# The epsilon of every layer norm added by VectorE instead of GpSimd, in a transformer block on one core

## The chip, the cores and the metric

The kernel runs on one core of a Trainium2 chip. The metric is the device time of one execution in microseconds (us), as the median of three runs. Five engines work side by side: TensorE (PE in the profile, its weight loads PEld), VectorE (DVE), ScalarE (ACT), GpSimd (POOL) and SyncE (SP), whose queue issues nearly all DMAs here. Each engine takes its instructions strictly in the order in which they were written, and waits on semaphores for the others.

## The reference

One block of a transformer over 2048 tokens of width 576, in bf16: a layer norm, an attention with 32 heads of width 18 in 4 segments of 512 tokens with a memory carried from segment to segment, a residual, a second layer norm, and a feed-forward network of width 4608 with gelu, and a second residual. Cut to what matters:

```
def _layernorm(x, axis=-1, eps=1e-05):
    m = mean(x); v = var(x)
    return (x - m) / sqrt(v + eps)

h   = x + A(_layernorm(x), wq, wk, wv, wo, beta)      # attention, 4 segments of 512 tokens
out = h + gelu(_layernorm(h) @ w1 + b1) @ w2 + b2
```

In A each segment s computes softmax(q k^T * scale + causal mask) v, mixed by a gate g = sigmoid(beta) with phi(q) M / (phi(q) z), where M and z sum phi(k)^T v and phi(k) over the segments before.

## The kernel before, in words

Tokens lie on the 128 partitions, so the 2048 tokens are 16 tiles of 128, four to a segment. Both layer norms are done tile by tile: 16 for the input x (stage X), 16 for h behind the attention (stage B), 32 in all.

The stages of a segment are X (layer norm of x and transposes to xreg; tiles of segment 0 and half of those of segment 1 are transposed on TensorE, L738, the others by DMA), P (projections to q, k, v, nine pairs of matmuls each, L835), A (scores L1002 and L1163, exponentials on ScalarE L1005 and L1167, masks on VectorE L1015 and L1176 or on GpSimd L1018 and L1178, values L1034 and L1189, block transposes on VectorE such as L1048, L1143 and L1197, and small normalising steps), M (the memory, L928), B (output projection L793 and L819, residual L1241, layer norm, transposes), C (first feed-forward matmul, L1301 and L1338, its evictions and the gelu) and D (second feed-forward matmul L1388, the last residual L1400, the store).

A layer norm of one tile is a small function, `layernorm` (L700 onward). It acquires one of six small buffers `ln` of 16 floats per partition and records three operations:

- `stats` on VectorE: two BN_STATS over the halves of 288 columns (L710) into columns 0 to 11, and a BN_AGGR (L711) that makes the mean (column 12) and the variance (column 13).
- `rstd` on GpSimd: a TENSOR_SCALAR (L714) that adds 1e-5 to the variance into column 14, and a TENSOR_TENSOR (L715) that raises column 14 to the power -0.5, read from the constant column `mhalf`, into column 15.
- `apply` on VectorE: subtracts the mean and multiplies by column 15 (L726). For the first two tiles of segment 0 it only subtracts the mean (L724), and the factor is put in where the projections are evicted (L628, L632).

What sets the order of the work: a table of numbers, TIMETABLE, which gives every operation an engine and a place in one global row. Operations are emitted in the order of these numbers. A small planner (`schedule`) walks the same row with the costs that stand in the code and picks which buffer of a set each operation gets; it does not reorder. The compiler adds the semaphore waits.

Of the kernel before, what the change touches and what calls it, by code (L numbers as in the profile page):

```python
# [12 lines left out]
ALU = mybir.AluOpType  # L13
# [357 lines left out]
class Graph:  # L371
# [12 lines left out]
    def add(self, prio, cost, fn, after=(), acq=None, use=(), table=None, size=0, name=""):  # L384
        key = self.tag + name
        n = self.count[key] = self.count.get(key, -1) + 1
        acq = [b for b in (acq if isinstance(acq, list) else [acq]) if b is not None]
        op = Op(prio, cost, fn, after, acq, [b for b in use if b is not None], table, size, name)
        op.tag = self.tag
        op.start, op.eng = self.timetable[key, n]  # L390
        for b in op.use + acq:
            b.left += 1
        self.ops.append(op)
        return op
# [66 lines left out]
def kernel(  # L461
# [11 lines left out]
    nc = tc.nc  # L473
# [15 lines left out]
    EPS = 1e-5  # L489
# [107 lines left out]
    def build():  # L597
# [4 lines left out]
        add = gr.add  # L602

        def memset(prio, eng, cost, *aps, val=0.0, after=()):
            def fn(e):
                for ap in aps:
                    if e == "act":
                        nc.scalar.memzero(ap)
                    else:
                        VEC[e].memset(ap, val)  # L610
            return add(prio, {eng: cost}, fn, after, name="memset")
# [38 lines left out]
        half_ok = memset(-9, "dve", 0.1, mhalf[:], val=-0.5)  # L650
# [53 lines left out]
        def layernorm(prio, src, after, xsrc, dst_buf, dcost, extra=(), centred=None):  # L704

            sm = Buf(ln_s)

            def stats(e):
                for c in range(2):
                    nc.vector.bn_stats(out=sm.t[:, 6 * c:6 * c + 6], in_=src()[:, c * HALF:(c + 1) * HALF])  # L710
                nc.vector.bn_aggr(out=sm.t[:, 12:14], in_=sm.t[:, 0:12].rearrange("p (a b) -> p a b", b=6))  # L711
            a = add(prio, {"dve": 1.06}, stats, after, sm, [xsrc], name="stats")
            def rstd(e):
                nc.gpsimd.tensor_scalar(out=sm.t[:, 14:15], in0=sm.t[:, 13:14], scalar1=EPS, scalar2=None, op0=ALU.add)  # L714
                nc.gpsimd.tensor_tensor(out=sm.t[:, 15:16], in0=sm.t[:, 14:15], in1=mhalf[:], op=ALU.pow)  # L715
            b = add(prio, {"pool": 0.92}, rstd, [a, half_ok], None, [sm], name="rstd")

            if centred is not None:
                rstd_of[centred] = sm, b

            def apply(e):
                w = src().shape[-1]
                if centred is not None:
                    VEC[e].tensor_scalar(out=dst_buf.t[:, 0:w], in0=src(), scalar1=sm.t[:, 12:13], scalar2=None, op0=ALU.subtract)  # L724
                    return
                VEC[e].tensor_scalar(out=dst_buf.t[:, 0:w], in0=src(), scalar1=sm.t[:, 12:13], scalar2=sm.t[:, 15:16], op0=ALU.subtract, op1=ALU.mult)  # L726
            return add(prio, {"dve": dcost}, apply, [a, b if centred is None else None] + list(extra), dst_buf, [sm, xsrc], name="apply")
# [15 lines left out]
        def stage_X(s, prio):  # L743
# [3 lines left out]
            for tl in range(TPS):  # L747
                gr.tag = f"X{s}{tl // 2 if s == 0 else ''}"
                if s == 0:
                    if tl == 1:  # L750
                        w_ok["q"] = load_w(-7.4, "q", 0)
                        xs_pre.append(load_x(-7.3, 2))
                        xs_pre.append(load_x(-7.2, 3, xs_pre[2][0]))
                        for op in (xs_pre[2][1], xs_pre[3][1], w_ok["q"][0]):
                            held(op).after.append(x_gate)
                    xb, ld = xs_pre[tl]
                elif tl % 2 == 0:
                    xb, ld = load_x2(prio + 0.1 * tl, s * TPS + tl, [applied[3]])
                xn = Buf(xn_s)
                pl = prio + 0.1 * tl if s == 0 else X_PRIO + 0.3 * s + 0.05 * tl  # L760
                ap = layernorm(pl, lambda xb=xb, tl=tl: xb.t[:, tl % 2, :], [ld] + ([xs_pre[0][1], x0b] if s == 0 else []), xb, xn, 0.50, [], tl if (s, tl) in CENTRED else None)
                applied.append(ap)
                if (s, tl // 2) not in PE_X:
                    wr[tl] = load(prio + 0.1 * tl, lambda tl=tl: xnd[s][tl * P:(tl + 1) * P, :], lambda xn=xn: xn.t[:], 164e3, [ap], use=[xn])
                    continue
                buf, j = bufs[tl // 2], tl % 2
                even = transposes(prio + 0.1 * tl, xn, [ap], lambda buf=buf, j=j: buf.t[:, 0:KT, j * P:(j + 1) * P],
                                  None if j else buf, [buf] if j else [], name="TX", one=0.06 if s or tl else 0.108)
                odd = transposes(prio + 0.1 * tl, xn, [ap], lambda buf=buf, j=j: buf.t[:, KT:ND, j * P:(j + 1) * P], None, [buf], ND - KT, name="TX", c0=64, one=0.06 if s or tl else 0.108)
                odd.after.append(even)  # L770
                if j:
                    even.after.append(xn_ok[s, tl - 1][0])
                xn_ok[s, tl] = [even, odd]
# [451 lines left out]
        def stage_B(s, prio):  # L1225
# [3 lines left out]
            for tl in range(TPS):  # L1229
# [9 lines left out]
                for hf, c in enumerate(cc):  # L1239
# [3 lines left out]
                        [c, xb] + ([] if hf == 0 else [h]), name="hadd")  # L1243
                xn2 = Buf(xn2_s)
                ap = layernorm(p0, lambda h=h: h.t[:], [prev], h, xn2, 0.62, later)
                ap = add(p0, {"pool": 0.29, "dve": 0.22}, lambda e, xn2=xn2: VEC[e].tensor_copy(out=xn2.t[:, D:XW], in_=xn2.t[:, 0:64]), [ap], None, [xn2],
                         name="tail")
# [174 lines left out]
        def tri_fn(e):  # L1422
# [10 lines left out]
            out=t[:, :, :, Dh:Dh + 1], in_=ident[:].rearrange("p (a b c) -> p a b c", a=TPS, c=1), func=ACT.Copy, scale=0.0, bias=1.0),  # L1433
# [116 lines left out]
```

## Time and profile before

| What | Value |
|---|---|
| median of 3 runs | 447.14 us (446.17 to 448.74) |
| span of the profiled execution, first to last instruction | 444.7 us |
| TensorE busy | 431.7 us, 97% of the span |
| VectorE busy | 291.2 us, 65% |
| ScalarE busy | 296.7 us, 67% |
| GpSimd busy | 179.3 us, 40% |
| mean granted TensorE clock | 0.999 |

The span is the time from the first to the last instruction of the profiled execution; no other time of that execution is given, and the median lies 2.4 us above the span. Times below are places in that span, in microseconds from its start. A busy share is an average over stages with different limits: VectorE has 65% over the span, but far more in the first quarter and nearly nothing in the last. TensorE's matmuls are pipelined, so a busy TensorE is one that always has a matmul in flight.

### The profile page before, as it was taken

Reading aid. Unit: us, or ns where it says so; the run is one execution under the profiler, and the core shown is the slowest. Engines: PE = TensorE matmul, PEld = TensorE weight load, DVE = VectorE, ACT = ScalarE, POOL = GpSimd, SP = SyncE. Lnnn points to the kernel's source line nnn. Section 1 sums busy time; section 2 is a strip of 40 time slices with the busy share of each in tenths; the row PEclk is TensorE's granted clock in tenths of the full one; section 3 lists DMA queues with packets and bytes.
Section 4 is the critical chain, followed back from the end, with each engine's and each line's share of the span. In section 5 each row is a group of like instructions: output and inputs, shape, how many; then the busy total and the mean of one; then the engine's idle time right before and its main releaser. Section 6 shows DMA issues by size and latency. Waiting matters only on the chain.

```text
span 444.7 us, 12623 instructions
## 1 busy us (share of the span) xinstructions
PE 431.7 (97%) x5355; PEld 278.3 (63%) x5355; DVE 291.2 (65%) x636; ACT 296.7 (67%) x269; POOL 179.3 (40%) x312
## 2 busy tenths in 40 slices
PE   8888999998999999999999999999999999999997
PEld 5666677765676776664445766654457775446775
DVE  5889888999899988867777987837765121010011
ACT  5999999999878798686798966752684002556000
POOL 5776756457748435734236559440011000000010
PEclk9999999999999999999999999999999999999999
DMA  6779989999999945693863355805463461550030
GB/s 208 204 250 246 271 264 279 228 228 244 236 257 348 315 152 166 175 242 69 245 190 52 107 146 161 201 2 153 131 210 111 101 171 39 169 194 1 1 107 28
DMA packets 85274, 76.73 MB, mean 173 GB/s; under 512 B 62945, under 2 KB 72545, under 8 KB 85217
## 3 DMA queue, kind: packets, MB, share of 16 engines
q1 hardware_dynamic: 85072, 75.83, 63.3%
q8 instruction: 42, 0.69, 0.7%
q10 hardware_dynamic: 144, 0.09, 0.1%
q14 instruction: 16, 0.12, 0.1%
HBM read 42.08 MB, written 18.87 MB: 137 GB/s over the span
## 4 chain that ended last, share of the span: by engine, by line
PE 75%; DVE 7%; DMA 6%; ACT 6%; POOL 2%; issue 2%; SPq 1%; POOLq 0%; DVEq 0%; ACTq 0%
PE bank L1388 27%; PE bank L1301 21%; PE bank L835 9%; PE bank L1338 6%; DMA w1g<-in_B_w_dram 4%; PE bank L1163 3%; ACT hT L1355 3%; PE bank L1189 3%; PE bank L793 2%; DMA x<-in_A_x_dram 2%; ACT pt L1167 1%; PE bank L1002 1%; PE bank L819 1%; DVE ln L710 1%; POOL pt L1178 1%
## 5 line engine op out<-in xcount | busy, mean ns | idle before, releaser
L1167 ACT ACTIVATE pt<-bank 128x2048 bf16<-128x2048 f32 x60 | 112.7, 1878 | 30.4 <-PE bank L1163 25.1
L1388 PEld LDWEIGHTS <-hT 128*128 128x128 bf16 x1152 | 110.2, 98 | 34.5 <-issue 7.0
L1301 PE MATMUL bank<-xreg,w1g 64*128 64x512 bf16 x972 | 108.0, 376 | 0.2 <-DMA w1g<-in_B_w_dram 0.2
L1301 PEld LDWEIGHTS <-w1g 64*128 64x128 bf16 x972 | 46.2, 94 | 57.1 <-issue 2.3
L1388 PE MATMUL bank<-w,hT 128*128 128x288 bf16 x576 | 78.3, 286 | 0.0
L1388 PE MATMUL bank<-w_lo,hT 128*128 128x288 bf16 x576 | 78.0, 286 | 0.0
L835 PE MATMUL bank<-hT,xreg 64*128 64x288 bf16 x864 | 58.0, 283 | 1.1 <-DVE qk_pad L634 0.6
L1306 ACT ACTIVATE hT<-bank,b_col 128x512 bf16<-128x512 f32 x36 | 22.5, 689 | 46.0 <-PE bank L1301 46.0
L1178 POOL TENSOR_SCALAR_AFFINE_SELECT pt<-pt 128x512 bf16<-128x512 bf16 x58 | 42.0, 737 | 27.1 <-ACT pt L1167 26.9
L835 PEld LDWEIGHTS <-xreg 64*128 64x128 bf16 x864 | 41.6, 94 | 14.3 <-issue 5.0
L1400 DVE TENSOR_TENSOR ot<-bank,hc 128x288 bf16<-128x288 f32 x32 | 13.8, 448 | 52.2 <-PE bank L1388 51.1
L1316 DVE TENSOR_SCALAR hT<-bank,b_col 128x512 bf16<-128x512 f32 x49 | 34.9, 742 | 18.6 <-PE bank L1301 18.5
L1374 POOL TENSOR_TENSOR hc<-hc,b_bc 128x576 f32<-128x576 f32 x9 | 11.7, 1297 | 82.0 <-DMA hc<-hd 82.0
L1005 ACT ACTIVATE pt<-bank 128x2048 bf16<-128x2048 f32 x20 | 37.6, 1880 | 2.8 <-PE bank L1002 2.1
L1338 PE MATMUL bank<-xreg,w1g 64*128 64x256 bf16 x648 | 38.3, 269 | 0.6 <-DMA w1g<-in_B_w_dram 0.6
L1338 PEld LDWEIGHTS <-w1g 64*128 64x128 bf16 x648 | 31.3, 94 | 6.4 <-issue 2.7
L1374 DVE TENSOR_TENSOR hc<-hc,b_bc 128x576 f32<-128x576 f32 x7 | 5.6, 817 | 43.8 <-DMA hc<-hd 43.8
L1321 ACT ACTIVATE hT<-hT 128x8192 bf16<-128x8192 bf16 (+2 forms) x6 | 31.8, 5321 | 1.7 <-DVE hT L1316 1.6
L1314 ACT ACTIVATE hT<-bank,b_col 128x512 bf16<-128x512 f32 x23 | 15.1, 685 | 21.9 <-PE bank L1301 21.6
L1176 DVE TENSOR_TENSOR pt<-pt,tri 128x512 bf16<-128x512 bf16 x38 | 21.5, 569 | 4.7 <-ACT pt L1167 4.7
L1163 PE MATMUL bank<-qk 32*128 32x512 bf16 (+3 forms) x384 | 23.8, 300 | 0.2
L1349 DVE TENSOR_TENSOR hT<-bank,b_col 128x512 bf16<-128x512 f32 x32 | 21.0, 681 | 3.8 <-PE bank L1338 3.4
(117 smaller groups left out, 564.1 us busy)
## 6 DMA issues: line engine op xcount, KB each, us to landing
w1g<-in_B_w_dram SPq DMA_DIRECT2D x41, 576.0 KB, 5.0
qkd<-qk_pad SPq DMA_DIRECT2D x15, 512.0 KB, 3.9
hd<-h SPq DMA_DIRECT2D x16, 288.0 KB, 3.9
hc<-hd SPq DMA_DIRECT2D x16, 288.0 KB, 3.6
w_lo<-in_B_w_dram SPq DMA_DIRECT2D x3, 864.0 KB, 7.0
w<-in_B_w_dram SPq DMA_DIRECT2D x3, 864.0 KB, 11.1
xb<-in_A_x_dram SPq DMA_DIRECT2D x16, 144.0 KB, 4.2
x2d<-xn SPq DMA_DIRECT2D x14, 160.0 KB, 2.9
```

The source lines that it names most:

```text
L835: nc.tensor.matmul(out=out, lhsT=xTb.t[r, k, ts], rhs=wt[r, k, :], start=(k == 0), stop=(k == ND - 1))
L1005: ex = add(ps, {"act": 1.88}, lambda e: nc.scalar.activation(out=pt.t[:], in_=st.t[:], func=ACT.Exp, scale=scale), [sc], pt, [st], table=" ...
L1163: nc.tensor.matmul(out=st.t[:, i, off:off + n_], lhsT=qk[rows, 1, kt * P:(kt + 1) * P], rhs=qk[rows, 0, kt * P:L], start=True, stop=True, ...
L1167: ex = add(ps, {"act": 1.88}, lambda e, st=st, pt=pt: nc.scalar.activation(out=pt.t[:], in_=st.t[:], func=ACT.Exp, scale=scale), [sc], pt, ...
L1176: nc.vector.tensor_tensor(out=blk, in0=blk, in1=tri[:].unsqueeze(1).to_broadcast([P, 4, P]), op=ALU.mult)
L1178: nc.gpsimd.affine_select(out=blk, in_=blk, pattern=[[0, 4], [1, P]], compare_op=ALU.is_ge, fill=0.0, base=0, channel_multiplier=-1)
L1301: nc.tensor.matmul(out=cc[w].t[:], lhsT=w1.t[rows, k, q, :], rhs=x2T[s].t[rows, k, :], start=(k == 0), stop=(k == ND - 1))
L1306: ready_f[f + w] = [add(pf - 12, {"act": 0.68}, lambda e, f=f, w=w, cc=cc: nc.scalar.activation(out=hT[:, :, f + w, :], in_=cc[w].t[:].rea ...
L1316: nc.vector.tensor_scalar(out=dst, in0=src, scalar1=b, scalar2=None, op0=ALU.add)
L1321: ge = add(2.9, {"act": 0.42 * (f1 - f0) + 0.2}, lambda e, f0=f0, f1=f1: nc.scalar.activation(out=hT[:, :, f0:f1, :], in_=hT[:, :, f0:f1, ...
L1338: nc.tensor.matmul(out=cc[w].t[:, q * 2 * P:(q + 1) * 2 * P], lhsT=w1.t[rows, k, q, :], rhs=x2T[s].t[rows, k, ts], start=(k == 0), stop=(k ...
L1388: nc.tensor.matmul(out=c.t[:, 0:HALF], lhsT=hT[:, tl // 2, f, (tl % 2) * P:(tl % 2 + 1) * P], rhs=w2_c[ch][:, f - ch * WCH, hf * HALF:(hf ...
```

## The change

The addition of 1e-5 moves from `rstd` into `stats`: VectorE writes column 14 right behind the aggregation, and GpSimd is left with the power. The planner's costs are changed with it (`stats` from 1.06 to 1.13, `rstd` from 0.92 to 0.60). The timetable is not touched.

```
             def stats(e):
                 for c in range(2):
                     nc.vector.bn_stats(out=sm.t[:, 6 * c:6 * c + 6], in_=src()[:, c * HALF:(c + 1) * HALF])
                 nc.vector.bn_aggr(out=sm.t[:, 12:14], in_=sm.t[:, 0:12].rearrange("p (a b) -> p a b", b=6))
-            a = add(prio, {"dve": 1.06}, stats, after, sm, [xsrc], name="stats")
+                nc.vector.tensor_scalar(out=sm.t[:, 14:15], in0=sm.t[:, 13:14], scalar1=EPS, scalar2=None, op0=ALU.add)
+            a = add(prio, {"dve": 1.13}, stats, after, sm, [xsrc], name="stats")
             def rstd(e):
-                nc.gpsimd.tensor_scalar(out=sm.t[:, 14:15], in0=sm.t[:, 13:14], scalar1=EPS, scalar2=None, op0=ALU.add)
                 nc.gpsimd.tensor_tensor(out=sm.t[:, 15:16], in0=sm.t[:, 14:15], in1=mhalf[:], op=ALU.pow)
-            b = add(prio, {"pool": 0.92}, rstd, [a, half_ok], None, [sm], name="rstd")
+            b = add(prio, {"pool": 0.60}, rstd, [a, half_ok], None, [sm], name="rstd")
```

In the built program VectorE has 32 instructions more and GpSimd 32 fewer; the order of everything else, on all engines, is the same row for row. In the changed kernel the addition stands at L712. Two places show it. The first is VectorE in segment 0, where the layer norms of segments 1 and 2 (buffers ln) stand between the steps of the attention (t, r and o_nat are its small buffers, pt the probabilities); the difference there, with its + for the change:

```order
 L710 BN_STATS ln_103<-x_64 128x6 x2
 L711 BN_AGGR ln_103<-ln_103 128x2
+L712 TENSOR_SCALAR ln_103<-ln_103 128x1
 L1048 STREAM_TRANSPOSE t_89<-bank 128x512
 L1052 RECIPROCAL r_105<-t_89 128x16
```

The addition stands ahead of the block transpose L1048, which read nothing of the layer norm and used to follow the aggregation at once. The second place is GpSimd at the start of the program, with the first two layer norms (ln_99, ln_100) around the clearing of a buffer, qk_pad:

```order
 L696 CAST mark<-x_64 1x1
 L610 MEMSET qk_pad_130 128x64x14
-L714 TENSOR_SCALAR ln_99<-ln_99 128x1
 L715 TENSOR_TENSOR ln_99<-ln_99,mhalf 128x1
 L610 MEMSET qk_pad_131 128x64x14
```

The addition goes, and the power and the clearing behind it move up by one place.

## The prediction, written before the changed kernel was run

> **What bounds the kernel now.** I read the first table of the page first, then the stretches of the span, and then, for the stretches in which TensorE loses time, the waits and the timeline.
>
> ```profile
> span 444.7 us, 12623 instructions
> PE 431.7 (97%) x5355; PEld 278.3 (63%) x5355; DVE 291.2 (65%) x636; ACT 296.7 (67%) x269; POOL 179.3 (40%) x312
> ```
>
> TensorE is busy for 431.7 of 444.7 us. So the time is TensorE's own work, which the change does not touch, and 13.0 us in which it has nothing to do. The change can move the time only through those 13.0 us. GpSimd, which is relieved, has 40%. By stretches (columns: stretch, length, busy time and instructions of each engine):
>
> ```profile
> 22.00:46.00 24.00, 21.27 (x448) 15.66 (x445) 21.89 (x57) 22.14 (x30) 16.81 (x26) 1.00 0.94 254
> 46.00:83.00 37.00, 37.00 (x710) 27.49 (x710) 32.64 (x75) 34.51 (x31) 23.17 (x60) 1.00 1.03 261
> 83.00:110.00 27.00, 25.07 (x427) 17.32 (x423) 25.13 (x61) 26.43 (x25) 17.67 (x31) 1.00 1.00 231
> 158.00:190.00 32.00, 31.51 (x349) 21.06 (x346) 26.73 (x64) 26.72 (x16) 19.21 (x30) 1.00 0.63 170
> 247.00:272.00 25.00, 24.68 (x267) 16.33 (x266) 20.42 (x47) 19.82 (x14) 16.11 (x27) 1.00 0.52 139
> ```
>
> From 46 to 83 us TensorE is never idle, so nothing that VectorE does a little later in there costs time as long as it stays ahead of TensorE. From 22 to 46 us TensorE is idle for 2.73 us and VectorE for only 2.11: here VectorE is nearly full. Which of its rows TensorE waits for there, the waits tell:
>
> ```profile
> PE bank L1034 <- DVE pt L1015: 0.2, 1, 0.2
> PE bank L835 <- DVE t L1048: 0.5, 1, 0.5
> PE bank L928 <- DVE t L1048: 0.3, 1, 0.3
> ```
>
> These are three waits of TensorE for VectorE, at 35.2, 37.8 and 40.4 us, each for an instruction that stands behind the statistics of a layer norm in VectorE's row. The last one is the place where VectorE's lateness is handed to TensorE.
>
> **The change part by part: what one addition costs VectorE.** No 128x1 addition on VectorE stands in the trace. The nearest rows (last columns: busy us, mean ns of one):
>
> ```profile
> L1202 DVE TENSOR_SCALAR r<-r,omg_q 128x16 f32<-128x16 f32 x24 | 5.8, 242 | 0.9
> L1444 DVE TENSOR_SCALAR g_bc<-g_bc 128x32 f32<-128x32 f32 x1 | 0.2, 170 | 0.0
> L610 DVE MEMSET v_aug<- 128x128 bf16 x1 | 0.2, 165 | 1.3 <-PEq L1534 1.3
> L610 DVE MEMSET mhalf<- 128x1 f32 x1 | 0.1, 59 | 0.0
> ```
>
> The nearest is L1444: the same operation, an immediate added to f32 in SBUF, on 32 columns, 170 ns. The two memsets give the price of a column: (165 - 59)/127 = 0.83 ns. So one column should take 170 - 31 x 0.83 = 144 ns, and I take 0.14 us. The bounds are 0.06 us (the memset of one column, which reads nothing) and 0.24 us (L1202, which also fetches its scalar from a column).
>
> In the Trainium skill, VectorE: DVE Perf Modes (section The TRN2 errata) gives a VectorE instruction on SBUF data 58 cycles plus one per column in its table, and says that the measured fixed part is nearer 150 cycles; at 0.96 GHz that is 0.06 us by the table and 0.16 us by the measured part. The row L1444 stands with the second.
>
> What an instruction delays in the row behind it is not its duration alone:
>
> ```profile
> 29.64 0.21 DVE L711 BATCH_NORM_AGGREGATE ln<-ln 128x2 f32<-128x12 f32 x1
> 29.77 0.67 DVE L1048 STREAM_TRANSPOSE t<-bank 128x512 f32<-128x512 f32 x1
> 30.48 0.25 DVE L1052 RECIPROCAL r<-t 128x16 f32<-128x16 f32 x1
> ```
>
> L1048 does not depend on L711 and starts 0.13 us after it, while L711 still runs: an overlap of 0.08 us. L1052 depends on L1048 and starts 0.04 us after its end. The addition depends on the aggregation, so it starts 0.25 us after it (0.21 + 0.04), and what follows starts 0.14 - 0.08 after that. The next instruction comes 0.31 us behind the aggregation instead of 0.13: **0.18 us later for each layer norm** (0.10 to 0.28 by the bounds). For all 32 that is 5.8 us of VectorE's row.
>
> **What one addition less gives GpSimd, and the layer norm.** Where nothing is in the way (258 us):
>
> ```profile
> 258.81 0.21 DVE L711 BATCH_NORM_AGGREGATE ln<-ln 128x2 f32<-128x12 f32 x1
> 259.11 0.22 POOL L714 TENSOR_SCALAR ln<-ln 128x1 f32<-128x1 f32 x1 [2.34 <-DVE ln L711]
> 259.41 0.57 POOL L715 TENSOR_TENSOR ln<-ln,mhalf 128x1 f32<-128x1 f32 x1
> 260.02 0.87 DVE L726 TENSOR_SCALAR xn<-h,ln 128x576 bf16<-128x576 f32 x1 [1.00 <-POOL ln L715]
> ```
>
> From the end of the aggregation (259.02) to the start of the power (259.41) it is 0.39 us: 0.09 to cross to GpSimd, 0.22, and 0.08 between the two. Afterwards it is 0.04 + 0.14 + 0.09 = 0.27. So a layer norm whose `apply` waits for the power ends 0.12 us sooner (0.20 to 0.02 by the bounds), and GpSimd's row is 0.30 us shorter at each. The added time on VectorE is under its own wait there, which is 1.00 us long.
>
> **The sum, by places.** (1) *28 to 41 us.* Four aggregations stand in VectorE's row before the last of the three waits, at 29.64 (above), 33.12, 36.25 and 39.50:
>
> ```profile
> 33.12 0.21 DVE L711 BATCH_NORM_AGGREGATE ln<-ln 128x2 f32<-128x12 f32 x1
> ...
> 39.50 0.21 DVE L711 BATCH_NORM_AGGREGATE ln<-ln 128x2 f32<-128x12 f32 x1
> 39.67 0.71 DVE L1048 STREAM_TRANSPOSE t<-bank 128x512 f32<-128x512 f32 x1
> ```
>
> VectorE's own waits from 22 to 46 us end with one for TensorE at 25.1 us:
>
> ```profile
> DVE v_aug L632 <- PE bank L835: 0.3, 1, 0.3
> ```
>
> Behind it VectorE waits for nobody until 45 us, so the four delays add up: 4 x 0.18 = 0.7 us by the transpose of 39.67, for which TensorE waits. What hangs on it are the projections of L835 that follow in TensorE's row, and from 46 us on a TensorE without gaps carries the lateness on: **+0.7 us** (0.4 to 1.1).
>
> (2) *The start.* TensorE's first transposes wait for L724, the subtraction of the mean, which stands behind the addition now:
>
> ```profile
> 4.39 0.39 DVE L724 TENSOR_SCALAR xn<-x,ln 128x640 bf16<-128x640 bf16 x1
> 4.94 0.57 POOL L715 TENSOR_TENSOR ln<-ln,mhalf 128x1 f32<-128x1 f32 x1
> 5.46 0.84 POOL L610 MEMSET qk_pad<- 128x896 bf16 x1
> 5.78 0.71 DVE L724 TENSOR_SCALAR xn<-x,ln 128x640 bf16<-128x640 bf16 x1
> 6.54 1.06 PE L738 MATMUL bank<-ident,xn 128*128 128x128 bf16 x9 [0.21 <-DVE xn L724]
> ```
>
> The first subtraction has cover, since TensorE is still in its warm-up matmuls. The second ends at 6.49 and TensorE follows at 6.54. Two additions stand ahead of it; L724 need no longer wait for the aggregation itself, so the second costs about 0.14 - 0.08 = 0.06, and with 0.1 from the first that is +0.16. Against it: L724 takes 0.71 us here, twice what the first one took (0.39 at 4.39), and ends 0.19 us after GpSimd's clearing of 5.46 to 6.30. If it was held by that clearing, a shorter row on GpSimd frees it sooner, by 0.1 to 0.3. I take **+0.1** (-0.2 to +0.2).
>
> (3) *99 to 106 us.* TensorE's values wait at 104.5 us for a copy behind L726, and L726 waits for the power:
>
> ```profile
> 101.29 0.64 DVE L1127 SCALAR_TENSOR_TENSOR e<-e,r 128x512 bf16<-128x512 bf16 x1
> 101.46 0.55 POOL L714 TENSOR_SCALAR ln<-ln 128x1 f32<-128x1 f32 x1 [1.09 <-DVE ln L711]
> 102.09 0.57 POOL L715 TENSOR_TENSOR ln<-ln,mhalf 128x1 f32<-128x1 f32 x1
> 102.70 0.88 DVE L726 TENSOR_SCALAR xn<-h,ln 128x576 bf16<-128x576 f32 x1 [0.40 <-POOL ln L715]
> 104.51 0.49 PEld L1189 LDWEIGHTS <-v_aug 128*19 128x19 bf16 x16 [0.77 <-DVE v_aug L634]
> ```
>
> L714 takes 0.55 us instead of 0.22, and ends 0.08 after L1127. Read as a hold by L1127, the power meets the same L1127, now 0.18 later, and ends where it ended or 0.1 later; read as chance, L726 starts up to 0.5 us sooner, as far as VectorE's row allows. I take **0** (-0.2 to +0.2). In the Trainium skill, SBUF — State Buffer (section Who interferes with whom) says that a VectorE instruction with two SBUF inputs and a GpSimd instruction that reads SBUF exclude each other, the second waiting in full; by that rule this term is 0 to +0.1, and without it -0.2; the stretched L714 agrees with the rule.
>
> (4) *158 to 190 and 247 to 272 us.* TensorE loses 0.49 and 0.32 us there. L726 waits for the power once in each, and 0.12 us comes back; but the delayed row of VectorE runs on to TensorE's waits behind. I take **-0.1** for both (-0.4 to +0.6). From 272 us on TensorE's idle time is not VectorE's, and the rest of the 32 additions lie under TensorE's work.
>
> Sum: 0.7 + 0.1 + 0 - 0.1 = +0.7 us. The profiled span would go from 444.7 to 445.4; the median of the runs lies 2.4 us above the span, and I let that stand: 447.14 + 0.7, rounded to **447.8 us**. By the bounds of (1) to (4) it reaches from 446.7 to 449.2.
>
> **The rivals.** *A, slower: VectorE is the bound in all four stretches.* In the stretches shown from 22 to 46, 83 to 110, 158 to 190 and 247 to 272 us stand 4, 2, 4 and 3 aggregations, by the same stretches for L711 alone (its busy time and count):
>
> ```profile
> 22.00:46.00 24.00, 0.84 (x4) 1.00 0.94 254
> ...
> 83.00:110.00 27.00, 0.42 (x2) 1.00 1.00 231
> ...
> 158.00:190.00 32.00, 0.83 (x4) 1.00 0.63 170
> ...
> 247.00:272.00 25.00, 0.63 (x3) 1.00 0.52 139
> ```
>
> If VectorE hands every delay of these 13 to TensorE, it is 13 x 0.18 = 2.3 us, or 449.5; with L1202's 0.24 us for the addition 13 x 0.28 = 3.6, or 450.8. It decides where TensorE's waits for VectorE grow in all four. For it: VectorE has 93% in the second of them. Against it: TensorE's idle time in the last two is 0.8 us together, so there is room between them now. A has 0.14. The Trainium skill speaks for it in VectorE: DVE Perf Modes (section Rules for kernel authors), which asks for fewer VectorE instructions rather than fewer semaphores.
>
> *B, faster: the power is what ends last.* VectorE waited for L715 five times, 3.6 us in all, and gets 0.12 us at each, 0.6; the start gains 0.2, and the 0.7 of place (1) vanishes in the overlaps that I could not see, or is won back because GpSimd's masks and gate steps, 0.30 us sooner at each layer norm, free VectorE's held instructions. 447.14 - 0.8 = 446.3. Condition: L726 starts sooner at 102.7 and 260.0, and 40.4 us is no later. The row of L726's idle time:
>
> ```profile
>   POOL ln L715: 3.6, 5
> ```
>
> B has 0.24.
>
> *C, nothing arrives:* the shift of 0.7 us is swallowed at a later wait that does not move with TensorE, such as the load of w1g behind which L1338 waits at 140 us. Then 447.1, inside the forecast's own range. C has 0.15.
>
> **How the numbers follow.** The forecast has 0.47, C 0.15, B 0.24, A 0.14. What a measurement of this kernel can tell from no change is about 0.5%, 2.2 us: below 444.9 is faster, above 449.4 slower. The forecast and C lie within; B would have to be three times as large as worked out to pass the bound, so of its 0.24 I put 0.06 there; of A's 0.14 I put 0.11 above the bound. That makes 0.06 faster, 0.83 the same, 0.11 slower. The range of 8 in 10 takes the forecast's bounds, B's value at the lower end and the beginning of A at the upper: 446.0 to 449.6.
>
> **What would show it.** L712 at 0.14 us, starting 0.04 after L711; the instruction behind it 0.31 us after the aggregation; L715 0.27 us behind L711's end at the layer norm of 258 us; VectorE's sum up by 32 x 0.14 = 4.5 us, GpSimd's down by 8.7 or a little more; TensorE's wait for L1048 at 40.4 us up from 0.5 to about 1.2, and its busy time unchanged. I am wrong if that wait has not grown, or if TensorE's idle time grows from 110 us on.

## The result, and the profile after

The changed kernel takes 449.15 us in the median (447.48 to 451.01, 20 runs), the kernel before 447.16 us beside it (445.79 to 448.74, 20 runs). The ratio is 1.0036 with an interval of 1.0023 to 1.0048: **1.6 us slower (1.0 to 2.1)**, the ratio less one times 447.2. That is within the 0.5% that I had called "the same" and inside the range, but more than twice the +0.7 us of the sum. The two medians lie 2.0 us apart; in what follows, microseconds against the kernel before are worked out from the ratio, which comes with an interval.

The profiled execution after has a span of 447.3 us and took 449.05 us. In the runs whose span is on record the time is about 1.75 us above the span, so the profile before, with 444.7, is an execution of about 446.4 us, 0.7 below the median of its kernel. The two profiles therefore lie 2.5 us apart (444.75 and 447.25, unrounded), where the ratio says 1.6.

The first table of the page and one group of instructions (last columns: busy us, mean ns, idle time before them), after:

```profile
PE 431.6 (96%) x5354; PEld 279.7 (63%) x5355; DVE 297.1 (66%) x668; ACT 297.0 (66%) x269; POOL 172.2 (39%) x280
L715 POOL TENSOR_TENSOR ln<-ln,mhalf 128x1 f32<-128x1 f32 x32 | 19.5, 613 | 31.8 <-DVE ln L712 28.8 <-DVE xn L1246 2.5 <-DVE mhalf L610 0.4
```

TensorE's work is what it was (431.7 before). Its idle time went from 13.0 to 15.7 us. GpSimd's sum fell by 7.1 us, less than the 8.7 that its additions took, mostly because the power, 575 ns on the mean before, now takes 613 (1.1 us more in all).

TensorE's waits for VectorE between 28 and 44 us, after:

```profile
PE bank L835 <- DVE t L1048: 1.6, 2, 1.0
PE bank L928 <- DVE t L1048: 1.2, 1, 1.2
```

The three waits shown of before add up to 1.0 us. Now it is 2.8, and no longer at the same places. TensorE's row in the timeline, after, shows where:

```profile
28.38 0.73 PE L1002 MATMUL bank<-qk 32*128 32x128 bf16 x16 [0.90 <-DVE xreg L634]
33.91 2.36 PE L835 MATMUL bank<-hT,xreg 64*128 64x288 bf16 x35 [0.98 <-DVE t L1048]
39.77 0.71 PE L928 MATMUL bank<-v_aug,fk_pad 128*128 128x76 bf16 x16 [1.18 <-DVE t L1048]
42.34 1.26 PE L835 MATMUL bank<-hT,xreg 64*128 64x288 bf16 x17 [0.65 <-DVE t L1048]
```

The wait at 33.9 us is new, and the one for L928 has grown from 0.28 to 1.18. The same matmuls stood at 27.93 (L1002), 37.78 (L928) and 40.43 us (the last L835) before. So TensorE is 0.45 us late when it enters this stretch, and 1.91 us late when it leaves it: **1.46 us are lost between 28 and 42 us.** The 0.45 us were there at 13 us already, behind the third transfer of weights, which landed at 10.27 us against 9.43 before; the last section shows that this landing scatters from profile to profile, so they are not put down to the change. Matched in the same way further on, the lateness is 2.29 us at 76.6, 2.17 at 104.5, 1.49 at 140, 2.60 at 144, 2.86 at 317 and 2.51 us at the end. Of the 2.51 us, the 1.46 from 28 to 42 us are the largest single piece.

**Where the 1.46 us come from.** Here are VectorE's rows and those of GpSimd beside them, first before, then after.

```profile
31.04 0.52 DVE L1057 TENSOR_TENSOR o_nat<-t,r 128x288 bf16<-128x288 f32 x1
31.33 1.20 POOL L1018 TENSOR_SCALAR_AFFINE_SELECT pt<-pt 128x1024 bf16<-128x1024 bf16 x1
33.50 1.12 POOL L1018 TENSOR_SCALAR_AFFINE_SELECT pt<-pt 128x1024 bf16<-128x1024 bf16 x1 [0.97 <-ACT pt L1005]
33.57 1.59 DVE L1015 TENSOR_TENSOR pt<-pt,tri 128x1024 bf16<-128x1024 bf16 x1
36.38 0.40 DVE L726 TENSOR_SCALAR xn<-x,ln 128x640 bf16<-128x640 bf16 x1
36.56 0.73 POOL L902 TENSOR_SCALAR rk<-qk_pad 128x576 bf16<-128x576 bf16 x1
37.66 0.72 DVE L726 TENSOR_SCALAR xn<-x,ln 128x640 bf16<-128x640 bf16 x1
```

```profile
30.09 0.21 DVE L711 BATCH_NORM_AGGREGATE ln<-ln 128x2 f32<-128x12 f32 x1
30.33 0.15 DVE L712 TENSOR_SCALAR ln<-ln 128x1 f32<-128x1 f32 x1
30.41 0.72 DVE L1048 STREAM_TRANSPOSE t<-bank 128x512 f32<-128x512 f32 x1
31.62 1.10 POOL L1018 TENSOR_SCALAR_AFFINE_SELECT pt<-pt 128x1024 bf16<-128x1024 bf16 x1
31.73 1.31 DVE L1057 TENSOR_TENSOR o_nat<-t,r 128x288 bf16<-128x288 f32 x1
33.94 1.10 POOL L1018 TENSOR_SCALAR_AFFINE_SELECT pt<-pt 128x1024 bf16<-128x1024 bf16 x1 [1.21 <-ACT pt L1005]
35.28 0.68 DVE L1015 TENSOR_TENSOR pt<-pt,tri 128x1024 bf16<-128x1024 bf16 x1
37.03 0.67 POOL L902 TENSOR_SCALAR rk<-qk_pad 128x576 bf16<-128x576 bf16 x1
37.37 1.40 DVE L726 TENSOR_SCALAR xn<-x,ln 128x640 bf16<-128x640 bf16 x1
37.64 0.95 POOL L610 MEMSET MZ_blk<- 128x1024 bf16 x1
```

The addition itself is as worked out: it starts 0.03 us behind the aggregation, takes 0.15 us, and L1048 comes 0.32 us behind the aggregation instead of 0.13. That is 0.19 us for each layer norm, 0.76 us for the four here.

The rest is a matter of who is first. Before, L1057 started 0.29 us ahead of GpSimd's mask L1018 and took 0.52 us. After, it starts 0.11 us behind the mask, takes 1.31, and ends 0.32 us after the mask does. L726 started 0.18 us ahead of L902 before and took 0.40. After, L902 is first by 0.34, and L726 takes 1.40, through L902 and the clearing of MZ_blk behind it, to 0.18 us past that clearing's end. One race goes the other way: L1015 lost by 0.07 us before and took 1.59, while now it starts when the mask is done and takes 0.68. A second L726 shrinks from 0.72 to 0.40. Sum: 0.76 + 0.79 (L1057) + 1.00 (L726) - 0.91 (L1015) - 0.32 = 1.32 of the 1.46.

In the Trainium skill, SBUF — State Buffer (section Who interferes with whom) says that a VectorE instruction with two SBUF inputs excludes a GpSimd instruction that reads SBUF, that one in a two-port mode excludes any, and that whoever issues first keeps the other out until it is done. VectorE's rows above agree: L1057, with two inputs, began 0.11 us behind the mask and ended 0.32 after it, and L726 ended 0.18 us after a clearing that reads nothing. Whether L726 runs in such a mode no run here shows. GpSimd's own delays are shorter than "until it is done" would make them: the mask that began 0.29 us behind L1057 took 1.20 us instead of 1.10, with 0.23 us of overlap, and L902 behind L726 0.73 instead of 0.67, with 0.22.

### The profile page after: what moved, and what is told of

It reads as the page before. It is cut to its first block, busy times and chain, and to the rows that moved or that the text cites. A ratio compares the mean times of both kernels' runs of the same rounds, so it can differ in the third digit from the quotient of the medians.

```text
span 447.3 us, 12620 instructions
## 1 busy us (share of the span) xinstructions
PE 431.6 (96%) x5354; PEld 279.7 (63%) x5355; DVE 297.1 (66%) x668; ACT 297.0 (66%) x269; POOL 172.2 (39%) x280
## 4 chain that ended last, share of the span: by engine, by line
PE 76%; DVE 13%; DMA 4%; issue 2%; POOL 2%; ACT 2%; SPq 0%; DVEq 0%; POOLq 0%; ACTq 0%
PE bank L1388 26%; PE bank L1301 22%; PE bank L835 8%; PE bank L1338 7%; PE bank L1163 3%; PE bank L793 3%; PE bank L1189 3%; DMA w1g<-in_B_w_dram 2%; DMA hT<-in_A_w_dram 1%; PE bank L1002 1%; DVE pt L1176 1%; DVE t L1143 1%; DVE xn L726 1%; DVE ln L710 1%; PE bank L819 1%
## 5 line engine op out<-in xcount | busy, mean ns | idle before, releaser
L835 PE MATMUL bank<-hT,xreg 64*128 64x288 bf16 x864 | 58.6, 283 | 2.9 <-DVE t L1048 1.6
L835 PEld LDWEIGHTS <-xreg 64*128 64x128 bf16 x864 | 43.2, 94 | 15.0 <-issue 7.0
L1178 POOL TENSOR_SCALAR_AFFINE_SELECT pt<-pt 128x512 bf16<-128x512 bf16 x58 | 41.8, 732 | 27.2 <-ACT pt L1167 27.0
L715 POOL TENSOR_TENSOR ln<-ln,mhalf 128x1 f32<-128x1 f32 x32 | 19.5, 613 | 31.8 <-DVE ln L712 28.8
```

Of the source, the lines that this page charges most:

```text
L835: nc.tensor.matmul(out=out, lhsT=xTb.t[r, k, ts], rhs=wt[r, k, :], start=(k == 0), stop=(k == ND - 1))
L1178: nc.gpsimd.affine_select(out=blk, in_=blk, pattern=[[0, 4], [1, P]], compare_op=ALU.is_ge, fill=0.0, base=0, channel_multiplier=-1)
```

## The experiments

Unless an edit says otherwise, each variant computes the same result, and the order of all other work is that of the kernel before. In variants with added lines the line numbers of the profile are some 1 to 4 higher (L1061 is L1057, L908 is L904), in e4 one lower. The expectations weigh three theories (row, collision, start), which the first of them explains. One measure serves for all: the length of VectorE's stretch from the start of L904 (28.13 us before) to the start of the last L1048 (39.67 us before), with the durations of three instructions in it, in us. It is read from the timeline of each variant's profile. What TensorE loses between the same places, matched matmul by matmul, is the growth of this stretch within 0.02 us in all 13 profiles. The stretch comes from one execution of a kernel and the time from 5 to 20, and the stretch is not the only place, so the two columns need not go together.

| kernel | time against before, us (interval) | stretch | L1057 | L1015 | first L726 |
|---|---|---|---|---|---|
| before | | 11.54 | 0.52 | 1.59 | 0.40 |
| the change | +1.6 (1.0 to 2.1) | +1.46 | 1.31 | 0.68 | 1.40 |
| e1_x2 | +0.8 (0.3 to 1.5) | +1.46 | 1.32 | 0.68 | 1.40 |
| e2_not_x2 | +0.8 (0.0 to 1.5) | 0 | 0.54 | 1.59 | 0.40 |
| e3_v_extra | +2.6 (1.5 to 3.8) | +1.49 | 0.46 | 0.68 | 1.74 |
| e4_p_less | -0.1 (-0.8 to 0.6) | +0.93 | 1.37 | 0.68 | 1.59 |
| e5_x0 | 0.0 (-0.6 to 0.6) | 0 | 0.52 | 1.59 | 0.40 |
| e6_twice | +2.2 (1.5 to 2.9) | +1.59 | 1.27 | 0.68 | 1.34 |
| e7_x2_v_extra | +1.6 (1.0 to 2.1) | +1.50 | 0.46 | 0.68 | 1.74 |
| e9_b123 | -0.2 (-0.8 to 0.4) | 0 | 0.52 | 1.59 | 0.40 |
| e10_after_moved | +0.8 (0.0 to 1.5) | +0.69 | 1.31 | 0.68 | 0.44 |
| e11_after_moved2 | +0.8 (0.1 to 1.5) | +0.38 | 0.46 | 0.68 | 0.44 |
| e12_before_moved2 | -0.1 (-0.8 to 0.6) | +0.09 | 0.52 | 1.59 | 0.40 |
| e13_b123_moved2 | 0.0 (-0.7 to 0.7) | +0.08 | 0.52 | 1.59 | 0.40 |

**Which layer norms cost the time.** The change is made for segment 2's four input layer norms alone (the four that stand between 28 and 41 us), or for the 28 others:

```
+            on_v = gr.tag == "X2"                # e2_not_x2: gr.tag != "X2"
...
+                if on_v:
+                    nc.vector.tensor_scalar(out=sm.t[:, 14:15], in0=sm.t[:, 13:14], scalar1=EPS, scalar2=None, op0=ALU.add)
...
+                if not on_v:
                     nc.gpsimd.tensor_scalar(out=sm.t[:, 14:15], in0=sm.t[:, 13:14], scalar1=EPS, scalar2=None, op0=ALU.add)
```

> The addition is on VectorE for the four layer norms of segment 2's input alone (those at 28 to 41 us); the other 28 stay on GpSimd. Row theory (VectorE's row from 28 to 41 us is full and hands each delay of 0.19 us to TensorE): +0.7 to +0.8 us against the kernel before, about half of the whole change, and L1057 and L726 of that stretch as long as before. Collision theory (the shift changes which VectorE and GpSimd instructions meet in the stretch, and one holds the other): +1.2 us or more, with L1057 near 1.3 us and one L726 near 1.4 us instead of 0.5 and 0.4. Start theory (the lateness comes from the first 12 us): within 0.2 us of before.

> The complement: the addition is on VectorE for 28 layer norms, and stays on GpSimd for the four of segment 2's input. Row theory: +0.8 us left (the change less 0.7 to 0.8). Collision theory: within 0.5 us of before if the collisions of 28 to 41 us fall as before. Start theory: +1.6 us, as the whole change.

Measured: e1_x2 448.21 us, 1.0019 (1.0006 to 1.0033); e2_not_x2 447.88 us, 1.0017 (1.0001 to 1.0033). The two add up to the whole. Four layer norms of 32 give the whole growth of the stretch and about half of the time. By their times alone both lie where the row theory put them, and e1's interval holds the collision theory's +1.2 as well. What speaks for the collisions in e1 is its profile: L1057 and L726 take 1.32 and 1.40 us, where the row theory had them as long as before. The other half, e2's, comes from a place that the prediction does not have. VectorE, GpSimd and TensorE at 17 to 20 us, e2_not_x2:

```profile
17.40 1.27 POOL L1022 TENSOR_SCALAR_AFFINE_SELECT pt<-pt 128x1024 bf16<-128x1024 bf16 x1 [0.41 <-ACT pt L1009]
17.62 1.66 DVE L908 SCALAR_TENSOR_TENSOR fk_pad<-ek,rk 128x576 bf16<-128x576 bf16 x1
19.66 1.52 PE L839 MATMUL bank<-hT,xreg 64*128 64x288 bf16 x22 [0.55 <-DVE xreg L634]
```

The kernel before has its L904 at 17.05 for 0.75 us, 0.38 ahead of the same mask. Two additions for segment 1's layer norms stand in VectorE's row just ahead of it (14.62 and 16.20 us here), and with them it comes 0.22 behind the mask, takes 1.66, and TensorE waits 0.55. Matched matmul by matmul, e2's TensorE is level with the kernel before at 17.4 us, 0.82 us late at 28 and 0.88 at the end, so this execution loses its time here; no experiment isolates the place. In the profile of the changed kernel itself this race was still won, with both starting at 17.9. But in e6 and e10, which make the whole change, L904 starts 0.17 and 0.16 us behind the mask and takes 1.66 and 1.67 us, and TensorE loses 0.87 and 0.80 us between 17 and 28. The changed kernel therefore probably wins this race in some executions and loses it in others, and its 1.6 us would be an average over both; that is argued, not shown.

**Segment 0, and the layer norms behind the attention.** The same selection for segment 0's four input layer norms, and for the twelve of segments 1 to 3 behind the attention:

```
+            on_v = gr.tag in ("X00", "X01")             # e5_x0
+            on_v = gr.tag in ("B1", "B2", "B3")         # e9_b123
```

> The addition is on VectorE for the four layer norms of segment 0's input alone (the first 14 us). Row theory: within 0.2 us of before, since the second subtraction L724 ends sooner (0.38 us instead of 0.71, as in the changed kernel) and TensorE then waits for the weights of q, which land when they land. Start theory (the new row at the start makes TensorE late by itself): +0.5 us or more.

> The addition is on VectorE for the 12 layer norms behind the attention of segments 1 to 3 alone, where L726 waits for the power at 174 and 260 us and VectorE has room. Row theory: -0.1 to -0.3 us, or nothing that can be told. Theory of rival A (VectorE is the bound from 158 to 190 and 247 to 272 us too): +0.5 us or more.

Measured: e5_x0 447.27 us, 1.0000 (0.9987 to 1.0013); e9_b123 446.81 us, 0.9995 (0.9983 to 1.0008). Neither can be told from no change. The twelve layer norms behind the attention, at 160 to 340 us, hand nothing on to TensorE that can be told. In the two stretches of theirs that the table by stretches before has, VectorE is busy for 82 to 84% (26.73 of 32 and 20.42 of 25 us), against 91% from 22 to 46 us (21.89 of 24).

**VectorE's addition without GpSimd's relief, and the reverse.** In e3_v_extra VectorE adds into a column that nobody reads any more, for all 32, and GpSimd keeps both its instructions. In e4_p_less the addition is left out altogether.

```
                 nc.vector.bn_aggr(out=sm.t[:, 12:14], ...)
+                nc.vector.tensor_scalar(out=sm.t[:, 0:1], in0=sm.t[:, 13:14], scalar1=EPS, ...)      # e3_v_extra
...
-                nc.gpsimd.tensor_scalar(out=sm.t[:, 14:15], in0=sm.t[:, 13:14], scalar1=EPS, ...)    # e4_p_less
-                nc.gpsimd.tensor_tensor(out=sm.t[:, 15:16], in0=sm.t[:, 14:15], in1=mhalf[:], op=ALU.pow)
+                nc.gpsimd.tensor_tensor(out=sm.t[:, 15:16], in0=sm.t[:, 13:14], in1=mhalf[:], op=ALU.pow)
```

> VectorE's half alone: all 32 layer norms have the addition on VectorE, into a column that nobody reads any more, and GpSimd still makes its own addition and the power. Row theory: +0.7 to +1.0 us, since GpSimd's relief plays no part. Collision theory: not the same as the whole change (over 0.5 us from it, either way), because GpSimd's instructions stand at other times against VectorE's.

> GpSimd's half alone: no addition at all, the power is taken of the variance itself, so the epsilon is left out of the computation. VectorE's row is as before. Row theory: -0.3 us (start and the waits for the power, as in rival B of the prediction). Collision theory: an effect of its own of 0.5 us or more, of either sign, from GpSimd's instructions that now start 0.3 us sooner and meet other VectorE instructions at 28 to 41 us.

Measured: e3_v_extra 449.85 us, 1.0059 (1.0033 to 1.0085); e4_p_less 447.23 us, 0.9998 (0.9983 to 1.0013). So the cost is VectorE's addition, and GpSimd's relief alone wins nothing that can be told. By its time e4 is a miss for the collision theory, which had 0.5 us or more, and fits the row theory's -0.3. Its profile shows more than that. VectorE has not one instruction more there, and its stretch is still 0.93 us longer. Its rows of VectorE and GpSimd at 30 us, and then e3's at 31 and 36 us:

```profile
30.38 1.10 POOL L1017 TENSOR_SCALAR_AFFINE_SELECT pt<-pt 128x1024 bf16<-128x1024 bf16 x1
30.43 1.37 DVE L1056 TENSOR_TENSOR o_nat<-t,r 128x288 bf16<-128x288 f32 x1
```

```profile
31.39 0.46 DVE L1058 TENSOR_TENSOR o_nat<-t,r 128x288 bf16<-128x288 f32 x1
31.40 1.41 POOL L1019 TENSOR_SCALAR_AFFINE_SELECT pt<-pt 128x1024 bf16<-128x1024 bf16 x1
36.70 0.67 POOL L903 TENSOR_SCALAR rk<-qk_pad 128x576 bf16<-128x576 bf16 x1
36.70 1.74 DVE L727 TENSOR_SCALAR xn<-x,ln 128x640 bf16<-128x640 bf16 x1
```

In e4 it is GpSimd that comes earlier (its mask starts at 30.38, 0.05 ahead, and its L902 at 35.69, 0.14 ahead of an L726 of 1.59 us), in e3 VectorE that comes later, and the same races are lost. In e3, L1057 wins by 0.01 us and the mask pays instead. The price is a matter of the order at each meeting, and the 0.19 us are only what changes it. That e4 is no slower for its longer stretch has two reasons in its profile. TensorE is 0.6 us ahead of the kernel before when it enters the stretch, as its weights at the start had landed early (9.22 us), which is chance as far as the last section shows. And it wins 0.33 us at 104.5 us and 0.37 between 260 and 272, places where the kernel before waits behind the power or for GpSimd's mask L1178. So in e4 GpSimd's relief wins at some places what it loses in the stretch.

**Twice the addition, and the extra addition for segment 2 alone.** In e6_twice VectorE adds a second time, into a column that nobody reads. e7_x2_v_extra is e3 for segment 2's input layer norms only.

> The whole change with a second VectorE addition behind the first, into a column that nobody reads: 0.23 us more on VectorE's row for each layer norm (0.15 of duration, 0.08 of overlap, since it need not wait), or 0.08 if the two overlap. Row theory: four times that from 28 to 41 us, so 0.3 to 0.9 us on top of the change, 2.0 to 2.6 us above before. Collision theory: not in step with the row; the instruction pairs that meet change again, so anything from 0.5 us below the change to 1.5 above it, with L1057 and L726 of 28 to 41 us at other durations than in the changed kernel.

> Only for the four layer norms of segment 2's input VectorE makes an extra addition that nobody reads; GpSimd is as before everywhere. Row theory: the same as with GpSimd relieved at these four, +0.7 to +0.9 us. Collision theory: L1057 comes first again (about 0.5 us instead of 1.3), as it did with the extra addition everywhere; what L726 does behind it decides: +0.8 us if it is free (0.4), +1.4 or more if it is held as there (1.7).

Measured: e6_twice 449.71 us, 1.0049 (1.0034 to 1.0065); e7_x2_v_extra 448.71 us, 1.0036 (1.0023 to 1.0048). The second addition, 144 ns, comes before the first one has ended and costs 0.07 us of VectorE's row. The stretch grows by 0.13 us over the change's and the time by 0.6 with overlapping intervals: no doubling. This time lies in the row theory's 2.0 to 2.6 us as well, so e6 does not tell the theories apart. e7, four instructions on one engine, measures as much as the whole change, with L1057 and L726 as the collision theory had them (0.46 and 1.74 us). But five of its eleven runs have a mean granted TensorE clock of 0.992 to 0.996; the other six, at 0.999 or 1.000, have a median of 448.3 us, 1.2 above the kernel before.

**Moving GpSimd's work out of the way.** If the meetings cost the time, two numbers of the timetable should win it back. They put the clearing of MZ_blk and L902 at other places of GpSimd's row; e12 and e13 make the moves of e11 in the kernel before and in e9.

```
-    "P1rk": "g 236 196 311 297",
+    "P1rk": "g 236 202.5 311 297",
...
-    "memset": "d1 d9 g25 g35 d0 a172 a7 a178 a68 g190 g200 g128",
+    "memset": "d1 d9 g25 g35 d0 a172 a7 a178 a68 g190 g212 g128",      # e10; e11, e12, e13: g176
```

> The whole change, with two GpSimd instructions that stood in the way of L726 at 37 us put later in GpSimd's row: the clearing of MZ_blk (0.95 us) and one L902 (0.67 us) come behind the combining steps L1057 instead of ahead of them. VectorE's row is the changed kernel's. Collision theory (L726 took 1.40 us instead of 0.40 because these two held it): L726 back at 0.4 us, 1.0 us less lateness by 40 us, +0.6 to +0.9 us above before instead of +1.6. Row theory alone (only VectorE's own instructions count): no better than the change, +1.6 us.

> As the run before, but the clearing stands ahead of the mask that collides with L1057 at 31.7 us, and so puts that mask behind L1057. Collision theory: L1057 back at 0.5 us and L726 at 0.4, 1.5 to 1.8 us less lateness by 40 us unless the mask, now 0.9 us later, holds another instruction; at or below the kernel before (-0.3 to +0.3 us). Row theory: +1.6 us.

> The kernel before with the same two moves in GpSimd's row: what the moves are worth without the change. In the kernel before L1057 (0.52) and the first L726 (0.40) were free already and only L1015 (1.59) and the second L726 (0.72) were held. Collision theory: -0.3 to -1.2 us, and the difference to the changed kernel with the moves is then the row's part alone, 0.7 to 0.8 us.

> The moves, with the addition on VectorE for the 12 layer norms behind the attention of segments 1 to 3 only: the version that should be the fastest by both theories, 0.1 to 0.3 us below the kernel before with the moves.

Measured: e10 447.97 us, 1.0017 (1.0001 to 1.0033); e11 448.10 us, 1.0018 (1.0003 to 1.0033); e12 447.26 us, 0.9998 (0.9983 to 1.0013); e13 447.25 us, 1.0000 (0.9985 to 1.0015). e10 came out as expected: with nothing of GpSimd beside it, L726 takes 0.44 us instead of 1.40, and the stretch grows by 0.69 instead of 1.46. The change costs about half of what it did, though the intervals overlap, and e10's profile has the lost race of L904 in it. e11 and e12 missed, and so did e13, which should have been the fastest. The rows of VectorE and GpSimd of the first two say why. First e11, then e12:

```profile
31.41 0.95 POOL L610 MEMSET MZ_blk<- 128x1024 bf16 x1
31.52 0.46 DVE L1057 TENSOR_TENSOR o_nat<-t,r 128x288 bf16<-128x288 f32 x1
33.74 1.10 POOL L1018 TENSOR_SCALAR_AFFINE_SELECT pt<-pt 128x1024 bf16<-128x1024 bf16 x1 [0.23 <-ACT pt L1005]
34.13 0.74 DVE L1053 TENSOR_TENSOR r<-r,omg_q 128x16 f32<-128x16 f32 x1
```

```profile
40.03 0.67 POOL L902 TENSOR_SCALAR rk<-qk_pad 128x576 bf16<-128x576 bf16 x1
40.20 0.54 DVE L634 CAST b_col<-ot 128x36 f32<-128x36 bf16 x1
40.65 0.70 DVE L1048 STREAM_TRANSPOSE t<-bank 128x512 f32<-128x512 f32 x1
```

With the clearing beside it L1057 is free (0.46 us), since the mask has gone elsewhere. There it meets L1053, a step of 16 columns that took 0.17 us and now takes 0.74. And L902, at its new place, meets a copy of 36 columns (L634, 0.13 us before, 0.54 now) that stands just ahead of the last L1048. Each move removed one meeting and made another. In e12 and e13, L1015 still loses its race and takes 1.59 us, which I had expected to end. No version came out that beats the kernel before: e9 with 446.81 is not told apart from it.

## Why the prediction was right or wrong

**The sign and the bound: right.** The change is slower, by less than the 0.5%, and TensorE's waits for VectorE from 28 to 42 us carry the largest part of the loss in the profile, with its busy time unchanged. What I had named as proof against me at 40.4 us did not occur: that wait grew, from 0.52 to 0.65. But the greater growth is in the two waits ahead of it, so even this sign stood at the wrong matmul. The other proof against me, idle time that grows from 110 us on, came true by a little: the lateness is 2.17 us at 104.5 and 2.51 at the end.

**L712 and the row: right.** 154 ns on the mean against 144 worked out, starting 0.03 us after the aggregation against 0.04; the next instruction 0.32 us behind the aggregation against 0.31; 0.19 us for each layer norm against 0.18. At 258 us in the old profile, 261 in the new, the timeline after:

```profile
261.50 0.21 DVE L711 BATCH_NORM_AGGREGATE ln<-ln 128x2 f32<-128x12 f32 x1
261.74 0.15 DVE L712 TENSOR_SCALAR ln<-ln 128x1 f32<-128x1 f32 x1
261.98 0.55 POOL L715 TENSOR_TENSOR ln<-ln,mhalf 128x1 f32<-128x1 f32 x1 [2.52 <-DVE ln L712]
262.56 0.87 DVE L726 TENSOR_SCALAR xn<-h,ln 128x576 bf16<-128x576 f32 x1 [0.66 <-POOL ln L715]
```

L715 starts 0.27 us behind the aggregation's end (261.71), as worked out, and VectorE's wait falls from 1.00 to 0.66. VectorE's sum grew by 5.9 us where I had 4.5, of which 4.9 are the additions.

**Term (1), +0.7: the step that failed.** "The four delays add up: 4 x 0.18." The 0.76 us of them are there, but the stretch grew by 1.46, outside the term's own 0.4 to 1.1. The step took every other instruction of VectorE's row to last as long as before. The profile before had the warning in it: L726 at 0.40 and at 0.72 us, and L1015 at 1.59 us, in one and the same stretch. I read such a pair as a hold at the start of the program and at 101 us, where it gave me the bounds of terms (2) and (3), and did not look for it where the largest term lay. Margins of 0.29 and 0.18 us, with delays of 0.19 us adding up one after the other, were there to be read. e4, which loses the same races without an added instruction on VectorE, and e10, which wins one back by moving GpSimd's steps alone, show the mechanism in their profiles. That the time lies inside the stated range all the same is owed to the room that the other terms and rival A had put into it.

**Term (2), +0.1 at the start: 0.0 (-0.6 to 0.6) in e5, but not for the reasons given.** The second L724 does take 0.38 us instead of 0.71, and TensorE's first projections start at 7.25 us against 7.64. But the earlier start is not owed to it: e1, e9, e12 and e13, whose segment 0 is unchanged and whose second L724 takes 0.70 or 0.71, start them at 7.22 to 7.29. Then they wait for weights. TensorE's row, after:

```profile
7.25 2.38 PE L835 MATMUL bank<-hT,xreg 64*128 64x288 bf16 x36
10.31 0.91 PE L835 MATMUL bank<-hT,xreg 64*128 64x288 bf16 x12 [0.68 <-DMA hT<-in_A_w_dram]
```

What the sum lacks is the next place, L904 at 17 us, where e2, e6 and e10 lose a race. It has no term, so of the 1.6 us about half stands at a place that the prediction did not look at.

**Term (3), 0 at 99 to 106 us: right, within its bounds.** TensorE's lateness goes from 2.25 us at 99.1 to 2.17 at 104.5. The power again meets L1127. Timeline after:

```profile
103.75 0.68 DVE L1127 SCALAR_TENSOR_TENSOR e<-e,r 128x512 bf16<-128x512 bf16 x1
103.92 0.92 POOL L715 TENSOR_TENSOR ln<-ln,mhalf 128x1 f32<-128x1 f32 x1 [1.15 <-DVE ln L712]
```

It takes 0.92 us instead of 0.57, so what the addition's leaving had freed went into the hold. The two halves of the change pull apart here: in e3's profile TensorE loses 0.30 us at this place, in e4's it wins 0.33.

**Term (4), -0.1: right as far as it can be seen.** In the profile the lateness falls by 0.02 us from 158 to 190 us and by 0.17 from 247 to 272. The second figure is 0.16 or 0.17 in all seven kernels that have VectorE's addition for the layer norm of 259 us without GpSimd's, and 0.01 at most in the five that leave that layer norm as it was or only add to it. e9's time gives -0.2 (-0.8 to 0.4).

**The rivals.** A falls with e9, as the late stretches hand nothing on, and with the lateness from 92 to 110 us, which is 2.16 at both ends. B, that GpSimd's relief wins time on the whole, falls with e4, although the relief does win 0.1 to 0.4 us at single places, as terms (3) and (4) show, and e3 (+2.6) against the change (+1.6) suggests that it is worth something once VectorE is late; their intervals overlap. C is half right: of the shift, the w1g load at 140 us gives back 0.65 us (the wait of 0.6 us there is gone after; one of 0.2 us for another load of w1g is new at 78.9). But a new wait for VectorE's L1349 takes 0.9 us at 144 us in its place. That wait stands also in e5, e12 and e13, which are no slower, so I don't count it as a cost of this change.

**Open.** Why e3 costs a microsecond more than e7, whose stretch is the same, was not settled: e3 has seven runs, 448.9 to 451.7 us, and its profile is of the fastest. In the profiles, 0.3 us of it stand at 104.5 us. The sum of e1 and e2 is placed only as far as one profile of each kernel can place it.

## What to carry to other kernels

On an engine's row that is nearly full, the cost of a small added instruction is its length plus what it changes at each meeting with an engine that can hold it. So ahead of the sum, look for instructions of one form with two durations in the profile, write down by how much each meeting is won or lost, and compare that margin with the accumulated delay; where the margin is smaller, the gap between the two durations belongs in the bounds. Work taken from the other engine shifts the same meetings, so it isn't a gain by itself. And a move that clears one meeting has to be checked at the place to which the work goes.

## What the runs showed that was not expected

- A step of VectorE as small as 16 or 36 columns can be held by GpSimd for 0.4 to 0.6 us: L1053 0.17 to 0.74 us (e11), L634 0.13 to 0.54 us (e12).
- L726, with one large input, waits also behind a clearing that reads nothing (1.40 us, to 0.18 past the clearing's end), while L1057, with two inputs, runs through beside one (0.46 us).
- The third weight transfer at the start was issued at 3.6 to 4.0 us in every profile and landed anywhere from 9.2 to 10.7 us, with no pattern by kernel (9.43 before, 10.27 after, 9.22 in e4, 10.70 in e12). TensorE's transposes L881 start 3.3 to 3.5 us behind it in 13 of the 14 profiles (3.7 in the kernel before), between 12.56 and 14.05 us. So the landing moves TensorE by up to 1.5 us, and is a likely, though not isolated, part of the 3 us by which runs of one and the same kernel differ.
